# Seven products instead of eight in the last matrix product, and a new order of pairs and weights in the stage ahead of it

## The chip, the cores and the metric

The kernel runs on one core of a Trainium2 chip. The metric is the device time of one execution in microseconds (us); the kernel before takes 1808.94 us (median of three runs, 1808.52 to 1811.02). TensorE (PE) multiplies matrices into PSUM, which has eight banks of 128x512 floats. ScalarE (ACT), VectorE (DVE) and GpSimd (POOL) prepare operands and clear PSUM. SyncE (SP) issues every DMA, in order. Each engine executes its own queue in the order in which the program was written.

## The reference

Attention with pooled keys and values feeds a first network, `_moe_ref`, and this a second one, `_moe2_ref`. The change touches the second alone, for 4608 tokens, 512 features and 1536 inner columns:

```python
def _moe2_ref(x, w_gate, w_val, w_out) -> np.ndarray:
    g = x @ w_gate
    silu = g * (1.0 / (1.0 + np.exp(-g)))
    val = x @ w_val
    return (silu * val @ w_out).astype(np.float32)
```

Weights arrive as 64-bit floats and are turned into 32-bit floats on the chip (`bits_ops`).

## The kernel before

Every product is computed from a high and a low part: an operand is split into `hi` (a rounded copy, made on ACT or DVE) and `lo` (the rest, a subtraction on DVE or POOL), and three matmuls (hi·hi, hi·lo, lo·hi) stand for one. Tokens are in nine tiles of 512.

Stage 1, to about 978 us, is attention and the first network. Stage 2, the gate stage, follows to 1511.85 us. There two token tiles make a pair; tile 8 is left over and makes a half pair of two pieces of 256 tokens. For a pair and one of six groups `g` of inner columns, the four products of a 2x2 block matrix (gate and value, for two token tiles) are computed by Strassen's scheme in Winograd's form as seven products (`PRODUCTS`): the left operands A11, A12, S1, S2, S3, A22, S4 are tokens or sums of them (`x_ops`), the right ones are weights or differences of them, prepared once in stage 1 by `conv2_ops` and kept in DRAM (`wdr`). Each of the seven takes 12 matmuls in a group (`pair_ops`). The weights of groups 0 to 2 stay in SBUF (21 slots, list `res`), those of groups 3 to 5 are loaded anew for every pair into four buffers X0 to X3 (`ring_load`), four products ahead. `u_ring` has eight tiles that take results out of PSUM; a finished tile goes to DRAM (`sdr`), and its buffer is free when the store has landed. Pairs run 0, 1, 2, 3, half; groups 0 to 5.

Stage 3 multiplies the results by `w_out` in the plain way: for each tile, 12 blocks `f` of inner columns, four blocks of features, three matmuls: 9·12·4·3 = 1296 of 512 columns, line 455 (`out_ops`, `mm3`). Its weights were split by `conv3_ops` (12 stores `wodr` of 512 KB) and are loaded at the end of the gate stage into the 12 first slots of `res`.

A list scheduler inside the program (`Plan`) writes the order of all queues. Each operation has a due time, alternatives by engine with assumed durations, and the operations it depends on; the scheduler takes what can start first, and among near equals what is due first. So an operation of low urgency runs as soon as its inputs and buffers are there. `at(when, ...)` sets only in which order buffers are handed out.

SBUF slots come from a lower and an upper region (`low`, and `const` or `al_p`). Token operands of stage 2 lie in the lower one (`x_ring`, 18 slots), as do X0 to X3 and the last two of the 21 slots; the other 19 slots lie in the upper.

Of the kernel before, what the change touches and what calls it, by code (L numbers as in the profile page):

```python
# [8 lines left out]
F32 = mybir.dt.float32  # L9
# [29 lines left out]
for _c in CHUNKS:  # L39
    for _t in range(2):  # L40
# [139 lines left out]
def tile_pooled_attention_moe_moe2(  # L180
# [358 lines left out]
    def conv2_ops(due, f):  # L539
        g, par = divmod(f, 2)  # L540
        (ta, ka), (tb, kb), (tg, kg), (tv, kv) = st_all[0:4]
        bits_ops(due, w_gate[f], kv_ring, Ring([(ta, ka), (tb, kb), (tg, kg)]))
        bits_ops(due, w_val[f], kv_ring, Ring([(ta, ka), (tb, kb), (tv, kv)]))
        h0, h1 = slice(0, 256), slice(256, 512)
        src = {"G1": (tg[:, h0], kg), "G2": (tg[:, h1], kg), "V1": (tv[:, h0], kv), "V2": (tv[:, h1], kv),
               "T1": (ta[:, h0], ka), "T2": (ta[:, h1], ka), "T3": (tb[:, h0], kb), "T4": (tb[:, h1], kb)}
        for o, x, y in (("T1", "V1", "G1"), ("T2", "V2", "T1"), ("T3", "V2", "V1"), ("T4", "G2", "T2")):
            (to, ko), (tx, kx), (ty, ky) = src[o], src[x], src[y]
            op(due, [e(256, lambda E=E, to=to, tx=tx, ty=ty: E.tensor_tensor(out=to, in0=tx, in1=ty, op=ALU.subtract))
                     for e, E in ((pool, P), (lambda n, fn: dve(n, fn, True), V))], [kx, ky], [ko])  # L550
# [70 lines left out]
    def pair_start(p, g):  # L621
        return P2S + p * NFP * P2D + g * (P2D if 2 * p + 1 < NTILE else P2L)

    scr = {}

    def pair_ops(p, g, j):
        n = TT if 2 * p + 1 < NTILE else TT // 2
        full = n == TT
        step = (P2D if full else P2L) / NPR
        k = p * NFP + g  # L630
        b1, b2, b3 = TURN[2 * k % 3], (5, 6), TURN[(2 * k + 1) % 3]

        def dst(i, f):
# [1 line left out]

        x, _, acc, first = PRODUCTS[j]
        for a in range(2):
            d = pair_start(p, g) + (j + 0.5 * a) * step
# [4 lines left out]
            for kk in range(2):  # L643
                kx, gx = xslot[p, x, kk]

                def product(kk=kk, bk=bk, gx=gx, gw=gw, a=a, first=first):
                    for q, (i0, i1) in enumerate(((0, 0), (0, 1), (1, 0))):
                        c = 256 * a + 128 * kk
                        nc.tensor.matmul(out=bk, lhsT=gw()[:, i0, c:c + 128], rhs=gx()[:, i1, 0:n],  # L649
                                         start=first and kk == 0 and q == 0, stop=kk == 1 and q == 2,  # L650
                                         skip_group_check=True)

                op(d, [pe(680 * n / TT, product)], [kw + "h", kw + "l", kx + "h", kx + "l"], [kb])
# [36 lines left out]
    out_slot = {}  # L690

    def out_ops(due, t, f, ring):
        (y, Y), (kg, gg) = ys_ring(), ring()
        keys = [f"sdr{t // 2}_{t % 2}_{f}"] if t < NTILE - 1 else [f"sdr{t // 2}_{i}_{f}" for i in range(2)]
        op(due - 1.5, [dma(1 << 18, lambda: sync.dma_start(out=ys(y), in_=sdr[t][f]))], keys, [Y])
        op(due - 0.5, [act(512, False, lambda: A_.copy(out=gg()[:, 0, :], in_=ys(y))),
                       dve(512, lambda: V.tensor_copy(out=gg()[:, 0, :], in_=ys(y)), True, 2)], [Y], [kg + "h"])
        op(due - 0.5, [dve(512, lambda: V.tensor_tensor(
            out=gg()[:, 1, :], in0=ys(y), in1=gg()[:, 0, :].bitcast(F32), op=ALU.subtract), True),
            pool(512, lambda: P.tensor_tensor(  # L700
                out=gg()[:, 1, :], in0=ys(y), in1=gg()[:, 0, :].bitcast(F32), op=ALU.subtract))],
           [Y, kg + "h"], [kg + "l"])
        kw, gw = out_slot[f]
        for dt in range(4):
            bi = 4 * (t % 2) + dt
            op(due, [pe(680, lambda dt=dt, bi=bi: mm3(
                bank[bi], gw(), slice(dt * 128, dt * 128 + 128), gg(), f == 0, f == NF2 - 1))],
               [kw + "h", kw + "l", kg + "h", kg + "l"], [f"bank{bi}"])
        if f == NF2 - 1:
            for dt in range(4):  # L710
                (z, Z), bk, kb = o_ring(), bank[4 * (t % 2) + dt], f"bank{4 * (t % 2) + dt}"
                op(due, [act(512, True, lambda z=z, bk=bk: A_.copy(out=z, in_=bk)),
                         dve(512, lambda z=z, bk=bk: V.tensor_copy(out=z, in_=bk))], [kb], [Z])
                op(due, [dma(1 << 18, lambda z=z, dt=dt: sync.dma_start(
                    out=outT[dt, :, t * TT:(t + 1) * TT], in_=z))], [Z], [f"out{t}_{dt}"])

    o_ring = Ring(st_all)


    groups = []  # L720
# [80 lines left out]
    for p in range(NP2):  # L801
        for q in range(2 * NPR):
            kk, o = divmod(q, NPR)
            if p == 0:
                w = LAST + 3.0 + 4.5 * kk + 0.6 * o
            else:
                w0 = pair_start(p - 1, NFP - 1)
                w = w0 + 0.01 if q < XSPARE else max(w, w0 + P2D / NPR * ((q - XSPARE) % NPR + 1) + 0.01)
            at(w, x_ops, w, p, kk, o, x_ring)
        for g in range(NFP):  # L810
            step = (P2D if 2 * p + 1 < NTILE else P2L) / NPR
            s0 = pair_start(p, g)
            if g >= RES:
                for j in range(NPR):
                    at(s0 + (j - 3.9) * step, ring_load, s0 + (j - 4) * step, g, j)
            for j in range(NPR):
                at(s0 + j * step, pair_ops, p, g, j)
    last = [wslot_k for _, wslot_k in res]
    for f in range(NF2):
        out_slot[f] = last[f]  # L820
        w = pair_start(NP2 - 1, f // NPR + 1) + 0.1
        at(w, load_ops, w, out_slot[f], wodr[f], [f"wodr{f}"])
    g_ring = Ring(last[NF2:n_up])
    for t in range(NTILE):
        for f in range(NF2):
            w = P3S + P3D * (t * NF2 + f)
            at(w, out_ops, w, t, f, g_ring)

    with tc.manual_schedule():
        A_.preload_act_table_set("natural_log_exp_and_others")  # L830
# [49 lines left out]
```

## Time and profile before

| | |
|---|---|
| median of three runs | 1808.94 us |
| the profiled execution | 1811.45 us |
| its span, first to last instruction | 1809.7 us |
| mean granted clock | 0.99 |
| PE busy | 1752.4 us (97%) |
| DVE, ACT, POOL busy | 1204.9, 1014.1, 468.0 us |
| DMA moved | 255.31 MB |

The profile comes from one execution, whose own time stands in the second row; 1.75 us of it lie outside the span. Times in the rows below count from the start of the span. A matmul's shown duration overlaps that of the next, so the pace is read from the starts of successive rows.

### The profile page before, as it was taken

To read this page: it belongs to the slowest core of one execution; us is meant where nothing else is said; L and a number is where in the kernel's file an instruction comes from. 1 tells how busy PE (TensorE), PEld (TensorE's weight loads), DVE (VectorE), ACT (ScalarE), POOL (GpSimd) and SP (SyncE) were. 2 spreads that over 40 slices of the span, in tenths; PEclk is the share of its full clock that TensorE was granted. 3 is DMA by queue.
4 is the path that set the end of the run, shared out by engine and by line. 5 is a ranking of instruction groups with operands and counts; after the bars stand their busy time and mean duration, and the time that the engine had idled before them with its cause. 6 is when DMAs were issued, how large, how long until landed. Compare 5 with 4: busy or idle time off the path is not lost.

```text
span 1809.7 us, 23566 instructions
## 1 busy us (share of the span) xinstructions
PE 1752.4 (97%) x8136; PEld 1414.1 (78%) x8136; DVE 1204.9 (67%) x1933; ACT 1014.1 (56%) x2184; POOL 468.0 (26%) x370
## 2 busy tenths in 40 slices
PE   5899899999999999999999999999999999999999
PEld 3577667787778877777888887888878888888887
DVE  7899988989889898988998435363453542222221
ACT  7777777778777777777876334343343332322222
POOL 4556542536443343524543001010000000000000
PEclk9799999999999999999999999999999999999999
DMA  8412353424132331313257374381653895434432
GB/s 273 145 41 82 113 158 104 133 71 145 48 126 88 104 120 55 122 35 134 95 196 268 134 248 141 132 275 47 221 186 104 268 325 188 144 118 122 142 120 70
DMA packets 117816, 255.31 MB, mean 141 GB/s; under 512 B 12224, under 2 KB 36800, under 8 KB 117696
## 3 DMA queue, kind: packets, MB, share of 16 engines
q1 hardware_dynamic: 117696, 253.81, 42.4%
q8 instruction: 64, 1.05, 0.2%
q14 instruction: 56, 0.46, 0.1%
HBM read 176.16 MB, written 77.59 MB: 140 GB/s over the span
## 4 chain that ended last, share of the span: by engine, by line
PE 83%; DVE 7%; DMA 5%; ACT 3%; issue 1%; POOL 1%; SPq 0%; DVEq 0%; ACTq 0%; POOLq 0%
PE bank L455 52%; PE bank L649 26%; PE bank L437 2%; PE bank L384 2%; PE bank L421 1%; DVE SC L517 1%; DVE G L514 1%; DMA ys_vps<-ydr 1%; DMA RAW<-in_k 1%; DVE SA L520 1%; DMA RAW<-in_v 1%; DMA X<-wdr 1%; DVE SA L509 1%; ACT QS L399 1%; DVE bank L510 0%
## 5 line engine op out<-in xcount | busy, mean ns | idle before, releaser
L455 PE MATMUL bank<-G,W 128*128 128x512 f32 x2088 | 515.0, 394 | 0.6 <-POOL W L324 0.6
L455 PEld LDWEIGHTS bank<-G,W 128*128 128x128 f32 x2088 | 387.3, 188 | 86.7 <-issue 5.2
L455 PE MATMUL bank<-X,W 128*128 128x512 f32 x1728 | 444.6, 402 | 7.3 <-DVE SA L520 7.1
L455 PEld LDWEIGHTS bank<-X,W 128*128 128x128 f32 x1728 | 322.9, 191 | 91.5 <-DVE SA L520 13.7
L506 POOL TENSOR_TENSOR SC<-SC,SB 128x512 f32<-128x512 f32 x144 | 201.9, 1402 | 290.3 <-ACT SC L504 288.6
L649 PE MATMUL bank<-W,X 128*128 128x512 f32 (+1 forms) x972 | 216.2, 367 | 5.9 <-DMA X<-wdr 3.0
L649 PEld LDWEIGHTS bank<-W,X 128*128 128x128 f32 x972 | 168.8, 188 | 38.4 <-ACT SA L658 1.8
L649 PE MATMUL bank<-W,W 128*128 128x512 f32 (+1 forms) x828 | 184.3, 367 | 0.4 <-ACT SB L658 0.4
L455 PE MATMUL bank<-W,W 128*128 128x512 f32 x756 | 174.0, 389 | 0.0
L649 PEld LDWEIGHTS bank<-W,W 128*128 128x128 f32 x828 | 143.8, 188 | 27.3 <-ACT SB L658 0.6
L455 PEld LDWEIGHTS bank<-W,W 128*128 128x128 f32 x756 | 141.9, 188 | 29.4
L512 ACT ACTIVATE SB<-SC,qc 128x512 f32<-128x512 f32 x144 | 104.8, 727 | 65.2 <-POOL SC L506 64.6
L514 DVE SCALAR_TENSOR_TENSOR G<-bank,ab,SB 128x512 fp32r<-128x512 f32 x144 | 107.2, 745 | 41.5 <-PE bank L455 28.6
L503 ACT ACTIVATE SB<-bank 128x512 f32<-128x512 f32 x144 | 86.3, 599 | 66.0 <-DVE G L525 41.2
L504 ACT ACTIVATE SC<-SB,babs 128x512 f32<-128x512 f32 x144 | 117.8, 818 | 0.1
L517 DVE SCALAR_TENSOR_TENSOR SC<-SC,G 128x512 f32<-128x512 f32 x144 | 114.0, 792 | 2.6
L507 ACT ACTIVATE SA<-bank,ab 128x512 f32<-128x512 f32 x144 | 112.3, 780 | 0.1
L510 DVE SCALAR_TENSOR_TENSOR bank<-SA,ab,bank 128x512 f32<-128x512 f32 x144 | 107.5, 747 | 1.3
L520 DVE SCALAR_TENSOR_TENSOR SA<-bank,ab,SC 128x512 f32<-128x512 f32 x144 | 106.6, 741 | 0.4
L320 POOL TENSOR_TENSOR ST<-ST,ST 128x512 int32<-128x512 int32 x53 | 77.0, 1453 | 114.0 <-DVE ST L317 78.4
L509 DVE TENSOR_TENSOR SA<-SA,bank 128x512 f32<-128x512 f32 x144 | 97.5, 678 | 10.3 <-ACT SA L507 9.6
L399 ACT ACTIVATE QS<-bank,MX 128x72 f32<-128x72 f32 x272 | 83.8, 325 | 35.1 <-DVE MX L395 35.1
(182 smaller groups left out, 2243.5 us busy)
## 6 DMA issues: line engine op xcount, KB each, us to landing
X<-wdr SPq DMA_DIRECT2D x105, 512.0 KB
wdr<-ST SPq DMA_DIRECT2D x84, 256.0 KB
ydr<-ST SPq DMA_DIRECT2D x44, 256.0 KB
RAW<-in_w_out SPq DMA_DIRECT2D x19, 512.0 KB
RAW<-in_k SPq DMA_DIRECT2D x32, 288.0 KB
RAW<-in_v SPq DMA_DIRECT2D x32, 288.0 KB
W<-wdr SPq DMA_DIRECT2D x18, 512.0 KB
ys_vps<-sdr SPq DMA_DIRECT2D x36, 256.0 KB
```

The costliest lines, as they stand in the source:

```text
L399: A_.activation(out=ss[:, 4 * i + j, :], in_=src[:, j, :], func=AF.Exp, bias=mx[:, 4 * i + j, :], accum_out=sm[:, 4 * i + j, :])
L455: nc.tensor.matmul(out=out, lhsT=w[:, i0, wc], rhs=x[:, i1, :], start=first and j == 0, stop=last and j == 2)
L504: op(d, [act(512, False, lambda: A_.activation(out=C, in_=Bt, func=AF.Identity, scale=babs[:, 1:2], bias=babs[:, 0:1]), 2)], [kB, "ab"], [kC])
L506: op(d, [pool(512, lambda: P.tensor_tensor(out=C, in0=C, in1=Bt, op=ALU.mult))], [kB], [kC])
L507: op(d, [act(512, True, lambda: A_.activation(out=A, in_=hb, func=AF.Identity, scale=ab[:, 3:4], bias=ab[:, 2:3]), 2)], [kh, "ab"], [kA])
L509: op(d, [dve(512, lambda: V.tensor_tensor(out=A, in0=A, in1=hb, op=ALU.mult))], [kh], [kA])
L510: op(d, [dve(512, lambda: V.scalar_tensor_tensor(out=hb, in0=A, scalar=ab[:, 1:2], in1=hb, op0=ALU.add, op1=ALU.mult), ptrs=1)], [kA], [kh])
L512: op(d, [act(512, False, lambda: A_.activation(out=Bt, in_=C, func=AF.Ln, bias=qc), 1)], [kC], [kB])
L514: op(d, [dve(512, lambda: V.scalar_tensor_tensor(out=gt[:, 0, :], in0=hb, scalar=ab[:, 0:1], in1=Bt, op0=ALU.add, op1=ALU.mult), ptrs=1)], ...
L517: op(d, [dve(512, lambda: V.scalar_tensor_tensor(out=C, in0=C, scalar=QC, in1=gt[:, 0, :].bitcast(F32), op0=ALU.add, op1=ALU.mult), True)] ...
L520: op(d, [dve(512, lambda: V.scalar_tensor_tensor(out=A, in0=hb, scalar=ab[:, 0:1], in1=C, op0=ALU.add, op1=ALU.subtract), ptrs=1)], [kC, k ...
L649: nc.tensor.matmul(out=bk, lhsT=gw()[:, i0, c:c + 128], rhs=gx()[:, i1, 0:n], start=first and kk == 0 and q == 0, stop=kk == 1 and q == 2, ...
```

## The change

- **Output products by the same scheme.** `conv3_ops` takes two blocks of `w_out` at a time and prepares seven right operands per group (`seven_ops`, now shared with `conv2_ops`): 42 stores of 256 KB take the place of 12 of 512 KB, through two half buffers (`late_ring`). `left3_ops` loads results from `sdr`, builds S1 to S4 and splits all seven left operands; `out_ops` does seven products per pair, each of 36 matmuls (two feature blocks, six groups, three parts), 1008 matmuls of 512 columns and 252 of 256. The 18 slots of `x_ring` hold the split operands of three products. The loads of left operands have rings of six buffers: K1 (A21), K2 (A22, then S), K3 (A11) and T (A12, A22, and A12 once more).
- **Gate stage.** The half pair runs fourth, pair 3 last. In these two the groups run 3, 0, 4, 1, 5, 2, so that a streamed group stands next to a resident one. Output weights are loaded (`load3_ops`) into each resident slot once pair 3 has used it for the last time.

```diff
+P2SEQ = (0, 1, 2, 4, 3)
+GSEQ = tuple((0, 1, 2, 3, 4, 5) if i < 3 else (3, 0, 4, 1, 5, 2) for i in range(NP2))
...
-    wodr = [dr_p.tile([128, 1024], F32, name=f"wodr{f}") for f in range(NF2)]
+    wodr = [[dr_p.tile([128, 2, 256], F32, name=f"wodr{g}_{j}") for j in range(NPR)] for g in range(NFP)]
...
+    rawf = [r.bitcast(F32).rearrange("p a t -> p (a t)") for r in RAW]
+    halves = [(rawf[i][:, 512 * c:512 * c + 512], f"raw{i}{'ab'[c]}") for i in range(NRAW) for c in range(2)]
+    late_ring = Ring(halves[4:6])
...
+    def conv3_ops(due, g):
+        a, b, t0, t1 = st_all[0:4]
+        bits_ops(due, w_out2[2 * g], late_raw, Ring([a, b, t0]))
+        bits_ops(due, w_out2[2 * g + 1], late_raw, Ring([a, b, t1]))
+        seven_ops(due, (t0, t1), ((0, 0), (1, 0), (0, 1), (1, 1)), (a, b), late_ring,
+                  lambda j: (wodr[g][j], f"wodr{g}_{j}"))
...
+        sums = {"S1": ("S", "A21", "S", ALU.add), "S2": ("S", "S", "A11", ALU.subtract),
+                "S3": ("A21", "A11", "A21", ALU.subtract), "S4": ("S", "T", "S", ALU.subtract)}
...
+                    for q, (i0, i1) in enumerate(((0, 0), (0, 1), (1, 0))):
+                        c = 256 * i0 + 128 * d
+                        nc.tensor.matmul(out=bk, lhsT=gw()[:, g % 2, c:c + 128], rhs=gx()[:, i1, 0:n],
+                                         start=first and g == 0 and q == 0, stop=g == NFP - 1 and q == 2,
+                                         skip_group_check=True)
```

PE at the start of the output stage, first in the kernel before. Names are output, token operand, weights; W3, W5, W7 are slots of the upper region, X4 to X7 and the first W of each row after lie in the lower.

```order
L649 MATMUL bank3_137<-W20_1175,X0_76 128x512 x3
L455 MATMUL bank0_134<-W27_1588,W3_118 128x512 x3
L455 MATMUL bank1_135<-W27_1588,W3_118 128x512 x3
L455 MATMUL bank2_136<-W27_1588,W3_118 128x512 x3
L455 MATMUL bank3_137<-W27_1588,W3_118 128x512 x3
L455 MATMUL bank0_134<-W29_1689,W5_119 128x512 x3
```

The same place in the changed kernel:

```order
L668 MATMUL bank3_137<-W20_1205,W28_1658 128x512 x3
L769 MATMUL bank0_134<-W22_1291,W3_118 128x512 x3
L769 MATMUL bank0_134<-W24_1408,W3_118 128x512 x3
L769 MATMUL bank0_134<-X4_80,W5_119 128x512 x3
L769 MATMUL bank0_134<-X5_81,W5_119 128x512 x3
L769 MATMUL bank0_134<-X6_82,W7_120 128x512 x3
L769 MATMUL bank0_134<-X7_83,W7_120 128x512 x3
L769 MATMUL bank1_135<-W22_1291,W3_118 128x512 x3
```

A bank now takes six groups in a row; one product needs six token operands, and weights of the upper region meet token operands of the lower.

ACT in the first pair of the gate stage, before: copies out of PSUM (L658), silu (L671, L679), and the preparation of the output weights (L532 makes a `hi` part; RAW2 is the buffer that is stored).

```order
L658 COPY SA0_95<-bank2_136 128x512
L532 CAST RAW2_103<-ST2_106 128x512
L658 COPY SA1_96<-bank3_137 128x512
L658 COPY SB0_97<-bank2_136 128x512
L658 COPY SB1_98<-bank3_137 128x512
L679 ACTIVATE bank2_136<-bank2_136 128x512
L679 ACTIVATE bank3_137<-bank3_137 128x512
L658 COPY SC0_99<-bank0_134 128x512
```

The same place after (L677 is the copy, L541 the `hi` part):

```order
L677 COPY SA0_95<-bank2_136 128x512
L541 CAST RAW2_103<-ST2_106 128x256
L677 COPY SA1_96<-bank3_137 128x512
L677 COPY SB0_97<-bank2_136 128x512
L541 CAST RAW2_103<-ST3_107 128x256
L321 ACTIVATE ST2_106<-RAW0_101 128x512
L677 COPY SB1_98<-bank3_137 128x512
L541 CAST RAW2_103<-ST0_104 128x256
L698 ACTIVATE bank2_136<-bank2_136 128x512
L698 ACTIVATE bank3_137<-bank3_137 128x512
L541 CAST RAW2_103<-ST0_104 128x256
L677 COPY SC0_99<-bank0_134 128x512
```

Such casts now stand between the copies up to the end of the third group: 22 of them on ACT from the first copy of the first pair on, 4 before.

SP in the half pair, before: W<-wodr loads output weights, sdr8 takes the half pair's results.

```order
L687 DMA sdr6_211<-SB1_98 128x512
L567 DMA W3_118<-wodr0_193 128x1024
L567 DMA W5_119<-wodr1_194 128x1024
L567 DMA W7_120<-wodr2_195 128x1024
L567 DMA W9_121<-wodr3_196 128x1024
L567 DMA W11_122<-wodr4_197 128x1024
L681 DMA sdr8_213<-SC0_99 128x256
L681 DMA sdr8_213<-SC1_100 128x256
L687 DMA sdr8_213<-SA0_95 128x256
L687 DMA sdr8_213<-SA1_96 128x256
L567 DMA W13_123<-wodr5_198 128x1024
```

SP in the half pair after, from its first stores on (X<-wdr loads streamed weights: group, then product):

```order
L700 DMA sdr8_243<-SA0_95 128x256
L584 DMA X0_76<-wdr4_2_181 128x1024
L700 DMA sdr8_243<-SA1_96 128x256
L706 DMA sdr8_243<-SC0_99 128x256
L706 DMA sdr8_243<-SC1_100 128x256
L584 DMA X1_77<-wdr4_3_182 128x1024
L608 DMA ys_vps_6796<-ydr6_148 128x512
L700 DMA sdr8_243<-ST4_108 128x256
L700 DMA sdr8_243<-ST5_109 128x256
L584 DMA X2_78<-wdr4_4_183 128x1024
L706 DMA sdr8_243<-SB0_97 128x256
```

The loads of output weights are gone from this stretch; they now come in pair 3.

## Rows read from the trace of the kernel before

**Rows 1.** The page, busy time by engine (us, share of span, instructions).
```profile
PE 1752.4 (97%) x8136; PEld 1414.1 (78%) x8136; DVE 1204.9 (67%) x1933; ACT 1014.1 (56%) x2184; POOL 468.0 (26%) x370
```
**Rows 2.** Busy time in four stretches (PE, PEld, DVE, ACT, POOL, clock, DMA).
```profile
985.00:1004.00 19.00, 19.00 (x84) 15.38 (x83) 11.14 (x19) 9.72 (x17) 3.46 (x3) 1.00 0.97 364
1329.00:1443.30 114.30, 114.30 (x503) 94.25 (x502) 49.67 (x81) 39.94 (x71) 1.29 (x2) 1.00 0.49 164
1443.30:1511.90 68.60, 63.23 (x506) 60.73 (x505) 28.34 (x69) 25.10 (x65) 2.15 (x2) 1.00 0.92 326
1511.90:1805.80 293.90, 293.90 (x1297) 243.09 (x1296) 74.42 (x112) 78.57 (x128) 0.00 (x0) 1.00 0.38 116
```
**Rows 3.** Chain that ended last, from 1443 us (start us, us, what).
```profile
1444.96 5.09 DMA sdr<-SB
...
1476.73 4.33 DMA sdr<-SC
...
1499.97 5.75 DMA X<-wdr
...
1512.01 293.81 PE bank L455 x1296
...
1805.88 0.59 ACT ST L712
```
**Rows 4.** Timeline of PE (start us, us, engine line op).
```profile
1245.42 9.09 PE L649 MATMUL bank<-W,W 128*128 128x512 f32 x39
1254.35 0.85 PE L649 MATMUL bank<-X,W 128*128 128x512 f32 x3
...
1445.79 3.34 PE L649 MATMUL bank<-W,W 128*128 128x256 f32 x27
1448.97 0.52 PE L649 MATMUL bank<-X,W 128*128 128x256 f32 x3
...
1475.99 0.52 PE L649 MATMUL bank<-X,X 128*128 128x256 f32 x3
1476.35 0.52 PE L649 MATMUL bank<-W,X 128*128 128x256 f32 x3
```
**Rows 5.** Groups by line and shape, 1100 to 1805 us (busy us, mean ns).
```profile
L663 DVE TENSOR_TENSOR SC<-SC,bank 128x512 f32<-128x512 f32 x28 | 19.0, 685 | 37.0 <-ACT SC L658 26.5 <-PE bank L649 8.2 <-ACT SC L671 2.0
L698 DVE TENSOR_TENSOR W<-ys_qs,W 128x512 fp32r<-128x512 f32 x23 | 15.8, 692 | 42.6 <-ACT W L696 42.6
...
L663 DVE TENSOR_TENSOR SB<-SB,bank 128x256 f32<-128x256 f32 x10 | 4.2, 418 | 10.0 <-ACT SB L658 10.0
...
L696 ACT CAST W<-ys_qs 128x512 fp32r<-128x512 f32 x23 | 14.3, 624 | 44.4 <-PE bank L455 44.0 <-PE bank L649 0.4
L658 ACT COPY SA<-bank 128x512 f32<-128x512 f32 x26 | 15.3, 587 | 33.9 <-PE bank L649 33.9
```
**Rows 6.** Timeline of SP: stores of gate operands, then the last stores of all.
```profile
711.77 11.91 SPq L555 DMA_DIRECT2D wdr<-ST  x5
...
737.41 13.04 SPq L555 DMA_DIRECT2D wdr<-ST  x4
...
813.66 16.60 SPq L555 DMA_DIRECT2D wdr<-ST  x7
...
1804.41 2.42 SPq L714 DMA_DIRECT2D outT<-ST  x4
```
**Rows 7.** Waits of PE, 1443 to 1512 us (us in total, times, longest).
```profile
PE bank L649 <- DMA X<-wdr: 3.0, 4, 1.3
PE bank L649 <- ACT SC L658: 1.1, 1, 1.1
```
**Rows 8.** Waits of PE in the full pairs, 1000 to 1443 us.
```profile
PE bank L649 <- ACT SA L658: 1.0, 2, 0.6
PE bank L649 <- ACT SB L658: 0.8, 2, 0.4
PE bank L649 <- ACT ST L658: 0.3, 1, 0.3
```

More of the change, by code (lines that the diff above doesn't have):

```diff
@@ L687, in pair_ops @@
                 op(d, [dma(512 * n, lambda t=t, f=f: sync.dma_start(out=dst(0, f), in_=t))], [kt], [f"sdr{p}_0_{f}"])
[L690 to L715, printed above, removed]
@@ L717, in tile_pooled_attention_moe_moe2, with s_load, left3_ops @@
-    o_ring = Ring(st_all)
+    rings3 = {}
+    s_live, a_slot, out_slot = {}, {}, {}
+    def s_load(due, p, nm, g, ring):
+        y, Y = rings3[ring]()
+        i, f = int(nm[1]) - 1, 2 * g + int(nm[2]) - 1
+        n = TT if 2 * p + 1 < NTILE else TT // 2
+        src = sdr[2 * p + i][f] if n == TT else sdr[2 * p][f][:, n * i:n * i + n]
+        op(due, [dma(512 * n, lambda: sync.dma_start(out=y()[:, 0:n], in_=src))], [f"sdr{p}_{i}_{f}"], [Y])
+        return lambda: y()[:, 0:n], Y
+    def left3_ops(due, p, j, g, slot):
+        n = TT if 2 * p + 1 < NTILE else TT // 2
+        nm, live = PRODUCTS[j][0], s_live.setdefault((p, g), {})
+        ld = due - 1.0
+        if nm == "A11":
+            live["A11"] = s_load(ld, p, "A11", g, "K3")
+        elif nm == "S1":
+            live["A21"], live["S"] = s_load(ld, p, "A21", g, "K1"), s_load(ld, p, "A22", g, "K2")
+        elif nm != "S2" and nm != "S3":
+            live["T"] = s_load(ld, p, "A12" if nm == "S4" else nm, g, "T")
+        sums = {"S1": ("S", "A21", "S", ALU.add), "S2": ("S", "S", "A11", ALU.subtract),
+                "S3": ("A21", "A11", "A21", ALU.subtract), "S4": ("S", "T", "S", ALU.subtract)}
+        if nm in sums:
+            (o, O), (x, X_), (y, Y), what = *(live[q] for q in sums[nm][:3]), sums[nm][3]
+            op(due, [e(n, lambda E=E: E.tensor_tensor(out=o(), in0=x(), in1=y(), op=what))
+                     for e, E in ((pool, P), (lambda n, fn: dve(n, fn, True), V))], [X_, Y], [O])
+        src, K = live[sums[nm][0] if nm in sums else "A11" if nm == "A11" else "T"]
+        k, get = a_slot[p, j, g] = slot
+        hi, lo = lambda: get()[:, 0, 0:n], lambda: get()[:, 1, 0:n]
+        op(due, [act(n, False, lambda: A_.copy(out=hi(), in_=src())),
+                 dve(n, lambda: V.tensor_copy(out=hi(), in_=src()), True, 2)], [K], [k + "h"])
+        op(due, [dve(n, lambda: V.tensor_tensor(out=lo(), in0=src(), in1=hi().bitcast(F32), op=ALU.subtract), True),
+                 pool(n, lambda: P.tensor_tensor(out=lo(), in0=src(), in1=hi().bitcast(F32), op=ALU.subtract))],
+           [K, k + "h"], [k + "l"])
@@ new lines, in load3_ops, with out_ops, product, copy @@
+    def load3_ops(due, j, g):
+        k, get = out_slot[j, g // 2]
+        c = g % 2
+        op(due, [dma(1 << 18, lambda: sync.dma_start(
+            out=get().bitcast(F32)[:, c, :], in_=wodr[g][j].rearrange("p h c -> p (h c)")))],
+           [f"wodr{g}_{j}"], [k + "hl"[c]])
+    def out_ops(p, j):
+        n = TT if 2 * p + 1 < NTILE else TT // 2
+        step = P3D if n == TT else P3L
+        _, _, acc, first = PRODUCTS[j]
+        b = [((3 * p + q) % 4 * 2, (3 * p + q) % 4 * 2 + 1) for q in range(3)]
+        for d in range(2):
+            due = P3B[p] + (j + 0.5 * d) * step
+            bi = b[acc][d]
+            bk, kb = bank[bi][:, 0:n], f"bank{bi}"
+            for g in range(NFP):
+                kx, gx = a_slot[p, j, g]
+                kw, gw = out_slot[j, g // 2]
+                def product(g=g, bk=bk, gx=gx, gw=gw, d=d):
+                    for q, (i0, i1) in enumerate(((0, 0), (0, 1), (1, 0))):
[3 more added lines that the diff above has]
+                                         skip_group_check=True)
+                op(due + 0.08 * step * g, [pe(680 * n / TT, product)], [kw + "hl"[g % 2], kx + "h", kx + "l"], [kb])
+            due += 0.5 * step
+            def copy(nm, bk=bk, kb=kb, due=due):
+                t, kt = u_ring()
+                scr[nm, d] = (t[:, 0:n], kt)
+                op(due, [act(n, True, lambda: A_.copy(out=t[:, 0:n], in_=bk)),
+                         dve(n, lambda: V.tensor_copy(out=t[:, 0:n], in_=bk))], [kb], [kt])
+            def add(nm, bi, due=due):
+                t, kt = scr[nm, d]
+                op(due, [dve(n, lambda: V.tensor_tensor(out=t, in0=t, in1=bank[bi][:, 0:n], op=ALU.add))],
+                   [f"bank{bi}"], [kt])
+            def store(nm, i, dt, due=due):
+                t, kt = scr[nm, d]
+                c = (2 * p + i) * TT if n == TT else 2 * p * TT + n * i
+                op(due, [dma(512 * n, lambda: sync.dma_start(out=outT[dt, :, c:c + n], in_=t))], [kt], [f"out{c}_{dt}"])
+            if j == 0:
+                copy("t0")
+            elif j == 1:
+                add("t0", bi)
+                store("t0", 0, d)
+            elif j == 3:
+                copy("v0")
+            elif j == 4:
+                copy("t1")
+                add("t1", b[2][d])
+                store("t1", 1, 2 + d)
+            elif j == 5:
+                copy("z")
+                store("z", 1, d)
+            elif j == 6:
+                add("v0", bi)
+                store("v0", 0, 2 + d)
@@ L816, in tile_pooled_attention_moe_moe2 @@
             for j in range(NPR):
[L817 to L827, printed above, removed]
+                at(s0 + j * step, pair_ops, i, c, j)
```

113 lines of the change are left out of this document (77 added, 36 removed).

## The prediction

> **What bounds the kernel now.** I read the page first: PE is busy 97% of the span [rows 1]. Then the stretches: in the last full pair and in the output stage PE fills its stretch, while DVE fills 49.67 of 114.3 us and 74.42 of 293.9 us [rows 2]; there the matmuls themselves are the time. The half pair is different: PE stands still for part of it, and the DMA engines are busy 0.92 of the time at 326 GB/s [rows 2]. The chain of waits says the same: from 1512.01 us it is one piece of 1296 matmuls, 293.81 us, and in the half pair it hops over DMA landings of 4.3 to 5.75 us [rows 3]. Last I read the pace of matmuls from the starts of successive rows. 39 matmuls of 512 columns with weights from the upper region and tokens from the lower take 1254.35 - 1245.42 = 8.93 us, 0.2290 us each [rows 4]; the output stage before has both operands in the upper region and takes 293.81/1296 = 0.2267 [rows 3]. With 256 columns it is (1448.97 - 1445.79)/27 = 0.1178 for weights from the upper region, and (1476.35 - 1475.99)/3 = 0.120 for streamed ones [rows 4]. The granted clock is 1.00, its upper level of 2.4 GHz, in all these stretches [rows 2]; I take it to stay.
>
> **Output stage.** Removed: 293.8 us. Added: per full pair 7 products of 36 matmuls, 252. By slots 19/21 of them (228) have weights of the upper region, so 0.2290, and 24 have 0.2267: 52.2 + 5.4 = 57.65 us; four pairs 230.6. The half pair has 252 of 256 columns, 29.7 us. Sum 260.3, **a gain of 33.5 us**, if nothing makes PE wait.
>
> The Trainium skill, page "TensorE: Matmul & The Clock Gate", section "Wait — 56ns, not 53.3ns?", puts the pace of a warm matmul at columns/2.4 GHz plus about 2.5 ns, thus 0.2158 and 0.1092 us. The rows here are 5 to 8% above that. By the page the gain would be 1296·0.2158 - 1008·0.2158 - 252·0.1092 = 34.6 us, an estimate 1.1 us above mine.
>
> What covers the added work: a full pair needs on DVE 42 `lo` parts, 20 of the 24 sums (the order gives the rest to POOL) and 6 adds from PSUM, 68 operations of at most 0.692 us [rows 5], 47 us beside 57.65; on ACT 42·0.624 + 8·0.587 = 31 us. DMA per pair: 36 loads and 8 stores of 256 KB, 11.5 MB in 57.65 us, 200 GB/s, under the 326 that the half pair moved [rows 2]. The 18 operand slots let the split work run up to two products, 16 us, ahead of PE, and a landing takes 4.3 to 5.8 [rows 3]. PE's accumulators are copied 4 us (half a product) before they are written again; a copy takes 0.59. So I expect little waiting: 1 us with the entry into the stage, bounds 0 and 4.
>
> The end gets shorter: before, four copies and four stores of 256 KB stand behind the last matmul, and 1809.7 - 1805.8 = 3.9 us pass [rows 3, 6]; after, one add of 0.42 and a store of 128 KB: -0.5 us.
>
> **Half pair.** It took 68.6 us [rows 2]; its 504 matmuls need 252·0.1178 + 252·0.120 = 59.9. Of the 8.7 lost, 3.0 are waits for streamed weights and 1.1 one wait for a result buffer (SC) whose store landed late [rows 3, 7]. The change takes 12 loads of 512 KB of output weights and the first loads of the output stage out of it; left are 21·0.52 + 24·0.13 MB of results + 8·0.26 of the next pair's tokens = 16.2 MB, 271 GB/s. Group order 3, 0, 4, 1, 5, 2 gives the first four loads of a streamed group a resident group's 9.9 us. But the last three can start only when the group's own products free a buffer: product 4's load starts after 12·0.118 = 1.4 us and is needed at 5.65. With 4.2 us to land, a landing of 5.75 [rows 3] costs 1.5 us per streamed group, 4.5 in all; a landing under 4.2 costs nothing. The long landings come from the fullest stretch; nearer the lower end I take 1.7. **Gain 7.0 us**, bounds 4.2 and 8.7.
>
> **Half pair to pair 3.** 14 operands of a full pair must now be split beside a group of 9.9 us instead of 19: 14 `lo`s and about 8 sums at 0.69 plus 10 operations of the group at 0.42 are 19.4 us on DVE; the new pair's first products (2.7 us each) give some of that time. The three full transitions before cost 2.1 us together [rows 8]. I add 1.0, bounds 0 and 19.4 - 9.9 - 2·2.7 = 4. In pair 3, streamed weights (11 MB), output weights (11), results (6.3) and first operands come to about 250 GB/s, no more than the half pair; each output load follows the product that frees its slot. Nothing added there.
>
> **Output weights (conv3).** 42 splits of 256 columns and stores of 256 KB replace 12 of 512 columns. Half of them run in tile 8 of stage 1, which has no attention work left, as their like, the 84 stores `wdr`, run in the tiles before it; nothing is set for that half. The rest stands in ACT's order in the first three groups of pair 0: 22 casts in 57 us, one per 2.6. Behind a cast that waits for its buffer stand PSUM copies, and PE wants the bank again after six matmuls, 1.4 us. The nearest rows for the pace of such a loop of two buffers are 16.60 us for seven stores and 11.91 for five, less the last issue (0.5): 2.7 and 2.85 us a store [rows 6]. 22·(2.85 - 2.6) = 5.5 us; if landings are as quick as assumed, nothing. The start of this stretch is full of other DMA (364 GB/s [rows 2]), so not nothing: **2.5 us lost**, bounds 0 and 5.7. A gain is excluded but for the 2.1 us of [rows 8], partly of this place.
>
> The Trainium skill, page "DMA: Bandwidth & Descriptors", section "Anatomy of one DMA — SWDGE (gpsimd) path", gives a DMA of that path about 2.0 us + bytes/436e3, 2.6 us for 256 KB. By that estimate the loop would need 1.7 us a store and this term would be nil; the rows of stage 1 are slower.
>
> **Sum**, against the profiled execution of 1811.45 us: -33.5 - 7.0 - 0.5 + 1.0 + 1.0 + 2.5 = -36.5. The median shown is 2.5 us under that execution: 1808.94 - 36.5 = 1772.4, **1772 us**.
>
> **Rivals.**
> - *Refills of T on the path (slower).* T's six buffers hold A12, A22 and A12 in turn, and SP is one strict queue in which these loads stand among stores that wait for DVE. If a refill starts only when PE is at the product before, its landing of about 5.1 us (the SB store of [rows 3]) shows twice per pair: 2·5·5.1 = 51 us, 1823 us. For it: six buffers for three uses. Against it: A22's split needs only the slot of a product three back, so the refill has 16 us. It decides from the point where the lead of 18 slots falls under one product, 8.2 us. Chance 0.04.
> - *DVE sets the pace in S1 to S4.* A product with sums needs 6 `lo`s, 6 sums, 1 add: 13·0.69 = 9.0 us against PE's 36·0.2290 = 8.2, for the half 13·0.418 = 5.4 against 4.2 [rows 5]. Three in a row overdraw 2.4 and 3.6 us a pair. If the lead of 16 us isn't there, 4·2.4 + 3.6 = 13: 1785 us. Against: the average is 47 of 57.65. Chance 0.07.
> - *The half pair's stall stays.* Were the streaming itself and not the output weights the cause, 7.0 us come back: 1779. The waits of [rows 7] for X<-wdr speak for it, the 6.3 MB taken out against. Chance 0.08.
> - *conv3 throttles pair 0.* One row shows four stores in 13.04 us, 4.2 each [rows 6]; at that pace 22·(4.2 - 2.6) = 35 us and 1805, no change. That row is of stage 1, where DVE is much fuller. Chance 0.03.
> - *My forecast* has the rest, 0.78.
>
> **Range and chances.** Without any of the waits that I added or left, and with 0.2267 for the output stage, it would be 1772 - 2.5 - 1 - 1 - 1.7 - 2.3, about 1764. With each at its upper bound 1772 + 3.2 + 3 + 3 + 2.8 = 1784. 1764 to 1784 leaves out T, DVE and conv3 and a little of the forecast. What a measurement can tell from no change is 0.2%, 3.6 us: faster 0.94 (forecast, DVE, half pair, a third of conv3), the same 0.02, slower 0.04.
>
> **What would show it.** The output stage: PE full, 252 matmuls in 57 to 58 us, with the two paces of [rows 4], and DVE at about 0.8. The half pair: 60 to 63 us, DMA share well under 0.92. Pair 0 of the gate stage: a few PE waits for L677 copies behind L541 casts, gone from the fourth group on. It is wrong if PE waits in the output stage for casts or `lo`s (DVE), if SP sits before a T load (T), or if waits for X<-wdr stay at 3 us and more.

## The result, and the profile after

The changed kernel takes 1779.5 us (median of four runs, 1777.7 to 1781.7) against 1810.0 beside it, a ratio of 0.983 (95% interval 0.9815 to 0.9849): 30.5 us faster. That is inside the range, 7.5 us above the forecast of 1772, and on the number of the rival "the half pair's stall stays" (1779). The profiled execution took 1777.68 us, its span 1775.9.

First the output stage, pair by pair (columns as in [rows 2]; the last stretch ends with the kernel):

```profile
1512.22:1569.90 57.68, 57.68 (x254) 47.37 (x253) 46.61 (x71) 30.38 (x51) 6.17 (x4) 1.00 0.69 236
1569.90:1627.50 57.60, 57.60 (x254) 47.30 (x253) 46.33 (x70) 30.46 (x51) 5.12 (x4) 1.00 0.62 201
1627.50:1685.20 57.70, 57.70 (x254) 47.40 (x253) 46.55 (x70) 30.57 (x51) 5.14 (x4) 1.00 0.61 199
1685.20:1742.80 57.60, 57.60 (x254) 47.30 (x253) 40.47 (x77) 26.35 (x49) 1.53 (x3) 1.00 0.43 136
1742.80:1775.90 33.10, 29.78 (x253) 29.57 (x251) 15.92 (x42) 11.69 (x33) 0.61 (x1) 1.00 0.20 65
```

PE is full in every pair, a pair takes 57.6 to 57.7 us, and DVE is busy at most 46.6 of them. Then the chain that ended last (start us, us, what), answering to [rows 3]:

```profile
766.06 13.95 PE bank L464 x60
...
1333.58 5.16 DMA X<-wdr
...
1344.01 4.86 DMA sdr<-SC
...
1356.99 5.23 DMA X<-wdr
...
1365.71 4.69 DMA sdr<-SA
...
1401.44 6.34 DMA X<-wdr
...
1512.38 260.21 PE bank L769 x1260
```

The output stage is one piece, 260.21 us in place of 293.81, but it begins where it began before, near 1512 us. The half pair, now from 1329.9 us, still hops over landings, of weight loads (X<-wdr) and of result stores (sdr) in turn. PE's waits there, 1329 to 1400 us (us in total, times, longest), beside [rows 7]:

```profile
PE bank L668 <- ACT SC L677: 2.4, 2, 1.3
PE bank L668 <- DMA X<-wdr: 2.3, 3, 1.0
PE bank L668 <- ACT SA L677: 0.7, 1, 0.7
```

The view behind [rows 7] has two more waits:

```profile
PE bank L649 <- ACT ST L658: 0.6, 1, 0.6
PE bank L649 <- ACT SB L658: 0.4, 1, 0.4
```

So before the change PE waited 2.1 us for copies into result buffers, not 1.1, beside 3.0 us for weights. The chain of [rows 3] has two more hops between those shown, and with them three result stores stand in it ahead of two weight loads:

```profile
1465.35 4.67 DMA sdr<-ST
...
1487.32 5.71 DMA X<-wdr
```

The DMA share of the half pair fell from 0.92 to 0.75, but that is a mean. While three of the landings in the changed kernel's chain were under way (columns as in [rows 2]), the DMA engines were busy nearly all the time:

```profile
1333.60:1338.70 5.10, 3.77 (x31) 3.40 (x29) 2.62 (x6) 2.72 (x7) 0.00 (x0) 1.00 1.02 341
1344.00:1348.90 4.90, 4.23 (x37) 4.02 (x36) 1.31 (x4) 0.84 (x2) 0.00 (x0) 1.00 0.91 256
1357.00:1362.20 5.20, 4.62 (x37) 4.24 (x36) 0.84 (x2) 1.72 (x6) 0.00 (x0) 1.00 0.98 314
```

To see where time went, I put marks into the two traces: M, a row of 60 matmuls of stage 1 near 767 us, which is in every trace (`766.06 13.95` above; 769.87 in the kernel before); E, the start of stage 1's last three matmuls; H, the start of the half pair's first matmul; O, the start of the output stage. In PE's timeline (columns as in [rows 4]) of the kernel before, E, the start of pair 3, the half pair's start (there after pair 3) and O:

```profile
989.11 0.86 PE L455 MATMUL bank<-G,W 128*128 128x512 f32 x3
...
1328.57 14.58 PE L649 MATMUL bank<-W,W 128*128 128x512 f32 x63
...
1443.32 0.52 PE L649 MATMUL bank<-X,W 128*128 128x256 f32 x3
...
1511.85 8.35 PE L455 MATMUL bank<-W,W 128*128 128x512 f32 x36
```

and of the changed one:

```profile
991.44 0.86 PE L464 MATMUL bank<-G,W 128*128 128x512 f32 x3
...
1324.43 9.91 PE L668 MATMUL bank<-W,X 128*128 128x512 f32 x60
...
1512.22 1.53 PE L769 MATMUL bank<-W,W 128*128 128x512 f32 x6
```

The row at 1324.43 us mixes sizes: by its length it holds 24 matmuls of 512 columns and 36 of 256, so H is 1324.43 + 24·0.2267 = 1329.9. Before, pair 2 ends where pair 3 begins, at 1328.57. H of the runs below is found the same way where a row mixes.

| stretch | before | after | difference |
|---|---|---|---|
| start to M | 769.9 | 766.1 | -3.8 |
| M to E, the end of stage 1 | 219.2 | 225.4 | +6.1 |
| E to the end of pair 2 | 339.5 | 338.5 | -1.0 |
| half pair and pair 3, in either order, to O | 183.3 | 182.3 | -1.0 |
| output stage | 294.0 | 260.4 | -33.6 |
| after the last matmul | 3.9 | 3.3 | -0.6 |

The first line is not the change's: no instruction differs there, and over all the runs below M stands anywhere from 764.4 to 772.6 us. Without it the two profiles differ by 30.0 us, as the medians do.

The other surprise of the table is +6.1 at the end of stage 1. Busy times from 885 to 990 us in the kernel before (columns as in [rows 2]):

```profile
885.00:990.00 105.00, 105.00 (x459) 85.89 (x458) 96.95 (x142) 78.13 (x124) 49.61 (x35) 1.00 0.58 197
```

and in the changed one:

```profile
885.00:990.00 105.00, 101.04 (x437) 81.36 (x436) 99.13 (x147) 72.75 (x120) 54.42 (x43) 1.00 0.59 195
```

PE's waits of the changed kernel, 900 to 990 us; the kernel before has none there:

```profile
PE bank L464 <- DVE SA L529: 3.6, 2, 2.1
PE bank L668 <- DVE SA L529: 0.4, 1, 0.4
```

DVE was already busy 97 of 105 us. It now takes 99, and twice it is so late with the activation of stage 1 that PE stands.

### The profile page after: what moved, and what is told of

It reads as the page before. It is cut to its first block, busy times and chain, and to the rows that moved or that the text cites. A ratio compares the mean times of both kernels' runs of the same rounds, so it can differ in the third digit from the quotient of the medians.

```text
span 1775.9 us, 24384 instructions
## 1 busy us (share of the span) xinstructions
PE 1715.5 (97%) x8100; PEld 1386.9 (78%) x8100; DVE 1356.4 (76%) x2204; ACT 1075.7 (61%) x2319; POOL 506.7 (29%) x406
## 4 chain that ended last, share of the span: by engine, by line
PE 80%; DVE 10%; DMA 5%; ACT 2%; issue 2%; POOL 1%; SPq 0%; DVEq 0%; ACTq 0%; POOLq 0%
PE bank L464 35%; PE bank L668 25%; PE bank L769 15%; PE bank L393 2%; PE bank L446 2%; PE bank L430 2%; DVE SC L526 1%; DMA ys_vps<-ydr 1%; DVE G L523 1%; DVE SA L529 1%; DMA X<-wdr 1%; DMA RAW<-in_k 1%; DVE SA L518 1%; DVE W L629 1%; DVE bank L519 1%
## 5 line engine op out<-in xcount | busy, mean ns | idle before, releaser
L464 PE MATMUL bank<-G,W 128*128 128x512 f32 x1728 | 430.9, 395 | 0.6 <-POOL W L333 0.6
L464 PEld LDWEIGHTS bank<-G,W 128*128 128x128 f32 x1728 | 319.7, 188 | 72.6 <-issue 5.2
L668 PE MATMUL bank<-W,W 128*128 128x512 f32 (+1 forms) x828 | 185.6, 367 | 1.8 <-ACT SC L677 1.1
L769 PE MATMUL bank<-W,W 128*128 128x512 f32 (+1 forms) x840 | 175.7, 366 | 0.0
L526 DVE SCALAR_TENSOR_TENSOR SC<-SC,G 128x512 f32<-128x512 f32 x144 | 117.1, 814 | 3.0
L529 DVE SCALAR_TENSOR_TENSOR SA<-bank,ab,SC 128x512 f32<-128x512 f32 x144 | 106.8, 742 | 0.4
L518 DVE TENSOR_TENSOR SA<-SA,bank 128x512 f32<-128x512 f32 x144 | 97.6, 679 | 9.9 <-ACT SA L516 9.5
```

The source lines that it names most:

```text
L464: nc.tensor.matmul(out=out, lhsT=w[:, i0, wc], rhs=x[:, i1, :], start=first and j == 0, stop=last and j == 2)
L518: op(d, [dve(512, lambda: V.tensor_tensor(out=A, in0=A, in1=hb, op=ALU.mult))], [kh], [kA])
L526: op(d, [dve(512, lambda: V.scalar_tensor_tensor(out=C, in0=C, scalar=QC, in1=gt[:, 0, :].bitcast(F32), op0=ALU.add, op1=ALU.mult), True)] ...
L529: op(d, [dve(512, lambda: V.scalar_tensor_tensor(out=A, in0=hb, scalar=ab[:, 0:1], in1=C, op0=ALU.add, op1=ALU.subtract), ptrs=1)], [kC, k ...
L668: nc.tensor.matmul(out=bk, lhsT=gw()[:, i0, m:m + 128], rhs=gx()[:, i1, 0:n], start=first and kk == 0 and q == 0, stop=kk == 1 and q == 2, ...
L769: nc.tensor.matmul(out=bk, lhsT=gw()[:, g % 2, c:c + 128], rhs=gx()[:, i1, 0:n], start=first and g == 0 and q == 0, stop=g == NFP - 1 and ...
```

## The experiments

Times are medians beside the kernel before on the same chip. Since the start scatters by 8 us, I read M to O, 746.2 us in the changed kernel and 742.0 before, as well. The last column is the half pair from its first matmul to its last, without six matmuls of the next stretch that stand among them; before the change it is 68.5. Both come from one execution of each kernel.

| kernel | median us | ratio (95% interval) | M to O | half pair |
|---|---|---|---|---|
| changed | 1779.5 | 0.9832 (0.9815 to 0.9849) | 746.2 | 66.4 |
| half pair fifth | 1782.2 | 0.9851 (0.9832 to 0.9870) | 750.5 | 69.9 |
| streamed groups first | 1783.5 | 0.9855 (0.9827 to 0.9883) | 748.1 | 68.3 |
| twelve result buffers | 1776.5 | 0.9822 (0.9798 to 0.9845) | 742.0 | 61.0 |
| half pair without streaming | 1772.0 | 0.9794 (0.9775 to 0.9813) | 741.4 | 59.6 |
| conversion after stage 1 | 1775.0 | 0.9820 (0.9797 to 0.9844) | 745.3 | 67.6 |
| no conversion | 1770.4 | 0.9784 (0.9769 to 0.9799) | 738.3 | 63.7 |
| three edits together | 1773.0 | 0.9799 (0.9775 to 0.9823) | 743.1 | 63.9 |
| before, twelve result buffers | 1811.3 | 1.0004 (0.9990 to 1.0017) | 740.0 | 68.8 |

**The gate stage's order.** My theory was that the new order had given nothing, the rival that it had given the 6 us of the prediction.

```diff
-P2SEQ = (0, 1, 2, 4, 3)
-GSEQ = tuple((0, 1, 2, 3, 4, 5) if i < 3 else (3, 0, 4, 1, 5, 2) for i in range(NP2))
+P2SEQ = (0, 1, 2, 3, 4)
+GSEQ = tuple((0, 1, 2, 3, 4, 5) for i in range(NP2))
```

> The changed kernel with the gate stage's order put back (half pair fifth, groups 0 to 5 in turn); output stage and output weights stay changed. Theory (the move gave almost nothing: half pair and pair 3 together take 182.5 us after and 182.8 before): 1779 to 1782 us, at most 2 above the changed kernel. Rival (the move gave the 6 us of the prediction, and something else lost them): 1785 to 1787 us.

> The changed kernel with the half pair fourth, but groups 0 to 5 in turn in it and in pair 3. Theory (the half pair stands still for result buffers and for loads queued behind stores on SP, which the group order does not touch): 1779 to 1781 us. Rival (the resident groups between give the streamed weights their time, as the prediction had it): 3 to 5 us above the changed kernel, 1783 to 1785 us, with waits for X<-wdr over 5 us in the half pair.

They took 1795.4 and 1799.9 us, far above either number, and answer another question. A last group that is streamed still needs X0 to X3 when the output stage puts its first operands there, so part of both is overwritten, and PE waits for the hand-over (12.6 us for X<-sdr in the second). The order is thus also what sets those four buffers free. So the place was put back alone:

```diff
-P2SEQ = (0, 1, 2, 4, 3)
+P2SEQ = (0, 1, 2, 3, 4)
```

> The changed kernel with only the order of the pairs put back: half pair fifth, groups 3, 0, 4, 1, 5, 2 in it and in the pair before it, so that its last group is a resident one and the four streaming buffers X are free for the output stage. Theory (the place is worth little, what the half pair stands still for is the loop of SP's queue and its result buffers): 1779 to 1782 us. Rival (the new output stage's first loads, 11 MB of weights and 18 operands, cost the half pair more than the old ones did): 1784 to 1790 us.

1782.2 us, at the upper end of the theory's range, and M to O 4.3 us longer. The half pair took 69.9 us there (1446.22 to 1516.1, the six output matmuls in its midst taken off). By these readings the place is worth some 3 to 4 us beside the new output stage; the intervals of the two medians overlap, so the size is not proven.

The half pair alone in turn, pair 3 alternating:

```diff
-GSEQ = tuple((0, 1, 2, 3, 4, 5) if i < 3 else (3, 0, 4, 1, 5, 2) for i in range(NP2))
+GSEQ = tuple((0, 1, 2, 3, 4, 5) if i < 4 else (3, 0, 4, 1, 5, 2) for i in range(NP2))
```

> The changed kernel with groups 0 to 5 in turn in the half pair alone (fourth, as changed); pair 3 keeps 3, 0, 4, 1, 5, 2. Theory (the alternation does nothing for the half pair): half pair and pair 3 take 182 to 184 us as with it (182.5), 1779 to 1781 us. Rival (resident groups between give streamed weights their time): waits for X<-wdr grow from 2.3 to over 5 us, 1782 to 1785 us.

1791.1 us, but no answer for a like reason: here the first loads of pair 3 take buffers that the half pair's last, streamed group has not read, and part of its result comes from other weights. The clean form ends on resident groups:

```diff
-GSEQ = tuple((0, 1, 2, 3, 4, 5) if i < 3 else (3, 0, 4, 1, 5, 2) for i in range(NP2))
+GSEQ = ((0, 1, 2, 3, 4, 5),) * 3 + ((3, 4, 5, 0, 1, 2), (3, 0, 4, 1, 5, 2))
```

> The changed kernel with the half pair's groups in the order 3, 4, 5, 0, 1, 2: still fourth and ending on a resident group, but its three streamed groups stand one behind the other. Theory (a streamed group needs a resident one beside it: 21 loads of 512 KB in 30 us would be 367 GB/s, more than the 326 that the old half pair moved): waits for X<-wdr grow from 2.3 us to 8 and more, half pair and pair 3 take 188 us and more instead of 182.5, 1785 us and more. Rival (the group order is worth nothing; the result buffers set the half pair's time in any order): 182 to 184 us, 1779 to 1781 us.

1783.5 us, a median between theory and rival, with half pair and pair 3 at 183.1. PE's waits, 985 to 1530 us, of which the half pair has those for X<-wdr alone:

```profile
PE bank L668 <- DMA X<-wdr: 6.7, 7, 1.7
PE bank L668 <- ACT ST L677: 1.0, 2, 0.8
PE bank L668 <- DVE SA L678: 0.7, 1, 0.7
```

Waits for weights grew from 2.8 us (2.3 in the half pair, 0.5 in pair 3) to 6.7, less than my theory's 8, and yet the stretch is only 0.8 us longer: the waits for ACT's copies that stood in the half pair, 3.1 us, are not there any more. One wait covers the other, and by that stretch the rival's 182 to 184 us fit.

**Result buffers.** If so, taking one away alone must show the other.

```diff
+    u_more = Ring(u_ring.items + st_all[0:4])
...
-                t, kt = u_ring()
+                t, kt = (u_more if i == 3 else u_ring)()
```

> The changed kernel with twelve result buffers instead of eight in the half pair (ST0 to ST3, idle there, join the ring). Theory (3.1 us of the half pair's standstill are copies that wait for a buffer whose store took 4.7 to 4.9 us to land): no wait for ACT's L677 copies is left in the half pair, its time with pair 3 falls from 182.5 by about 3, 1776 to 1777 us. Rival (behind them the streamed weights are late anyway): waits for X<-wdr take their place, 1779 to 1780 us.

Half pair and pair 3 fell from 182.3 to 176.9 us, 5.4 where 3 were expected, in one execution of each. PE's waits, 1331 to 1515 us:

```profile
PE bank L669 <- DMA X<-wdr: 1.6, 4, 0.7
PE bank L669 <- DVE SA L683: 0.2, 1, 0.2
```

No copy is awaited any more, the chain has no result store left in the half pair, and here the weights are not later but earlier. A reason that fits, and was not tried by itself: behind a store that waits for its data stand the next weight loads on SP's queue (the load at 1333.58 us above was issued right behind such a store), and stores are late where copies are. The median is 3 us lower, which its interval doesn't prove; M to O, read from one execution, is 4.2 us shorter. Streaming removed instead:

```diff
-            kw, gw = wslot[g, j]
+            kw, gw = wslot[g % RES if i == 3 else g, j]
...
-            if g >= RES:
+            if g >= RES and i != 3:
```

> The half pair's groups 3 to 5 take the resident weights of groups 0 to 2, so its 21 loads of streamed weights are left out and part of its result is another one. Theory (loads behind stores on SP's queue and the stores' landings beside them make the stall): the half pair falls to 60 to 61.5 us, with pair 3 to 175 to 177 instead of 182.5, 1772 to 1774 us. Rival (the result buffers alone make it): 3 us of waits for L677 stay, 1776 to 1777 us.

174.8 us with pair 3, 1772.0 us: as my theory had it. PE waits for ACT's copies 0.2 us there. So in these two traces either edit alone takes most of the stall: it needs both, the streamed loads and the few buffers. (The better version below gained less from the buffers.) In the kernel before the same twelve buffers:

```diff
-                t, kt = u_ring()
+                t, kt = (u_ring if full else u_more)()
```

> The kernel before with twelve result buffers instead of eight in its half pair, nothing else. Theory (the result buffers held its half pair too, but there the weight loads are late by themselves, at a DMA share of 0.92): the waits for L658 copies (2.1 us) go, those for X<-wdr stay at 3 or grow; the half pair falls from 68.6 to 65 or 67 us, 1806 to 1808 us. Rival (the result buffers are the whole cause): 62 to 63 us, 1803 to 1804. Rival (the weight loads are the whole cause, as the prediction had it): no change, 68 to 69 us.

No change: 1811.3 us, the half pair 68.8 (1438.24 to 1507.08) after 68.5. Waits of PE, 700 to 1815 us:

```profile
PE bank L650 <- DMA X<-wdr: 6.7, 7, 1.7
PE bank L650 <- ACT SB L659: 0.8, 2, 0.5
PE bank L650 <- ACT ST L659: 0.4, 1, 0.4
```

There the copies' waits in the half pair fell from 2.1 to 0.5 us, and the waits for weights grew from 3.0 us [rows 7] to 6.7: the weight loads are late by themselves. The waits went as the theory had it, but the time fits the last rival, the one that argued as the prediction did.

**The conversion of the output weights.**

```diff
-    at(P2S - 1, lambda: op(P2S - 1, [("NONE", 0, 0, False, lambda: None)], [], ["raw2"] + [k for _, k in halves[4:]]))
+    at(P2S + 3.9, lambda: op(P2S - 1, [("NONE", 0, 0, False, lambda: None)], [f"ydr{NTILE - 1}_3"],
+                           ["raw0", "raw1", "raw2"] + [k for _, k in halves[4:]]))
```

> The changed kernel with the output weights' conversion held back until the last tile of stage 1 is stored. Theory (in tile 8 its work takes time on a DVE that is 96% busy, and PE waits there 3.6 us for it): those waits are gone and pairs 0 to 2 carry the 42 splits with at most 2.5 us lost: 1774.5 to 1777 us. Rival (the conversion costs the same wherever it stands, by its loop of two buffers on ACT's and SP's queues): no change against the changed kernel, 1779 to 1782, the waits now in pairs 0 to 2.

M to E went back to 219.3 us, as before the change, and E to H grew from 338.5 to 342.8: 6.1 won, 4.3 lost, and the next stretch lost 0.9 more. In pairs 0 to 2 PE now waits 3.7 us for ACT's copies, 0.6 in the changed kernel. By M to O the rival is right, no change to speak of; the median of 1775.0, over runs from 1770 to 1783, can't decide. DVE's groups, 885 to 990 us (columns as in [rows 5], the idle time behind them), of the changed kernel and of this one:

```profile
L526 DVE SCALAR_TENSOR_TENSOR SC<-SC,G 128x512 f32<-128x512 f32 x18 | 17.1, 949 | 0.7
L529 DVE SCALAR_TENSOR_TENSOR SA<-bank,ab,SC 128x512 f32<-128x512 f32 x18 | 13.3, 741 | 0.0
...
L534 DVE TENSOR_TENSOR G<-SA,SB 128x512 fp32r<-128x512 f32 x15 | 12.3, 821 | 0.0
L518 DVE TENSOR_TENSOR SA<-SA,bank 128x512 f32<-128x512 f32 x17 | 11.5, 676 | 0.8 <-ACT SA L516 0.8
```
```profile
L526 DVE SCALAR_TENSOR_TENSOR SC<-SC,G 128x512 f32<-128x512 f32 x18 | 13.7, 760 | 0.9
...
L534 DVE TENSOR_TENSOR G<-SA,SB 128x512 fp32r<-128x512 f32 x18 | 13.5, 747 | 0.2
L529 DVE SCALAR_TENSOR_TENSOR SA<-bank,ab,SC 128x512 f32<-128x512 f32 x18 | 13.4, 746 | 0.1
...
L518 DVE TENSOR_TENSOR SA<-SA,bank 128x512 f32<-128x512 f32 x17 | 11.6, 682 | 2.2 <-ACT SA L516 2.2
```

The conversion doesn't only add operations to DVE. It also lengthens those that have both inputs in SBUF (L526 from 760 to 949 ns, L534 from 747 to 821), while those with an input in PSUM stay (L529, L518); POOL is busy 54 us of this stretch instead of 35. The price of all of it (only this hunk is printed; the loads of the output stage change too):

```diff
...
-    for g in range(NFP):
-        w = P2S + 4 + 9 * g
-        at(w, conv3_ops, w + 1, g)
```

> The conversion of the output weights is left out altogether; the output stage loads 256 KB blocks of the gate weights in their place, so only its time has a meaning. Theory: the 4.9 us that tile 8 lost come back, 1774 to 1775 us. Rival (tile 8's waits come from the order of the other work on DVE): 1778 to 1780 us.

1770.4 us: M to E 219.7, E to H 339.1, O 7.8 us earlier against M. Of that 5.7 us are at the end of stage 1; the rest shows in half pair and pair 3 (179.6). The theory was short by what lies past stage 1. The end of stage 1 is the firm part: M to E is 225.4 to 227.0 us in all nine traces in which the changed conversion starts in tile 8, and 219.2 to 219.7 in the other five, the two of the kernel before among them.

**Lead of the output stage.**

```diff
-                slot = x_ring.items[(2 * NPR * NP2 + pos) % len(x_ring.items)]
+                slot = x_ring.items[(2 * NPR * NP2 + pos % 12) % len(x_ring.items)]
```

> The changed kernel with 12 instead of 18 operand slots in the output stage, so that DVE's split work can run one product (8 us) ahead of PE instead of two. Theory (DVE overdraws 2.4 us in the three products with sums and makes it good in the other four; a lead of 8 us still covers that): output stage 260 to 263 us. Rival (the lead of 16 us is what hides DVE): PE waits for L742 parts in every pair, 265 to 275 us.

260.21 us for the stage, to the digit (1777.3 us, a single run). But this doesn't test the lead: operands are still handed out two products ahead, so with twelve slots they are written over ones not yet read, and the work runs as early as before. That the lead of two products is what hides DVE stays unshown. The run serves as a second one of the changed gate stage: half pair and pair 3 took 183.0 us, with 3.3 us of waits for copies and 2.9 for weights.

**A better version.** Held-back conversion with four staging buffers (RAW1 and RAW2) and twelve result buffers. RAW1 is taken from the loads of raw weights, which keep RAW0 alone; the lines of the other two experiments stand beside these:

```diff
-    late_raw = Ring(raw_all[0:2])
+    late_raw = Ring(raw_all[0:1])
...
-    late_ring = Ring(halves[4:6])
+    late_ring = Ring(halves[2:6])
...
```

> Three edits to the changed kernel together: the conversion of the output weights held back until stage 1 is stored, four staging buffers for it instead of two, and twelve result buffers in the half pair. Theory: tile 8 gives back 6 us and the half pair 5, as each alone did, and the four staging buffers bring the 4.3 us that the held-back conversion lost in pairs 0 to 2 down to 1: 1768 to 1770 us. Rival (the conversion costs pairs 0 to 2 by its casts in ACT's queue, not by its buffers): 4 us stay, 1772 to 1774 us.

1773.0 us, ratio 0.980: the lowest median of the kernels that compute everything, some 6 us under the changed kernel by ratio, though the intervals overlap, and 3 us by M to O. The rival's number fits. E to H is 341.8, so four staging buffers gave back 1 of the 4.3 us. PE's waits, 1331 to 1515 us:

```profile
PE bank L669 <- DMA X<-wdr: 4.2, 4, 1.6
PE bank L669 <- ACT W L627: 0.9, 1, 0.9
PE bank L669 <- ACT SC L678: 0.6, 1, 0.6
PE bank L669 <- DVE SA L683: 0.2, 1, 0.2
```

Here the half pair and pair 3 take 182.0 us, not 176.9, although no copy waits in the half pair (the 0.6 us for SC stand near the end of pair 3). Three of the four loads that were late are the same ones as with twelve buffers alone, each by 0.4 to 1.3 us more; the pair issued at 1400.57 us was awaited until 1407.29, there from 1400.39 to 1405.93. Whether that is the one execution or the moved conversion is open. Beside the held-back conversion with eight buffers (183.3) the twelve are worth 1.3 us, so the 5.4 above is no firm size: what the traces agree on is that with twelve buffers no copy waits in the half pair, and that late weights are then most of what is left.

## Why the prediction was right, and where not

- **Output stage, -33.5 and +1.0 for waits: right.** -33.6. The two paces of [rows 4] gave 57.65 us a pair, measured 57.6 to 57.7; no wait at all stood in the stage, so 1.0 was too careful. The rivals on T and on DVE are out: DVE's 46.6 us a pair is the 47 worked out, and nothing of it reached PE. (One reading was off without effect: the rows stand 5 to 10% above 0.2158 and 0.1092, not 5 to 8, since 0.120 is 10% above 0.1092.)
- **The end, -0.5:** -0.6.
- **Half pair, -7.0, and its transition, +1.0: the step that failed.** Together -6.0 expected, -1.0 measured. The half pair takes 66.4 us, not 61.6, and pair 3 after it about 1 us more than before. The step booked all of the 8.7 us but 1.7 as late weight loads that would go with the output weights' 6.3 MB. It put the waits for result buffers at nothing without a reason, and it saw 1.1 us of them where the trace had 2.1. They stayed: 3.1 us, beside 2.3 for weights. The buffers come free when their stores have landed, and stores on the chain still took 4.7 to 4.9 us: the step reasoned with a mean (271 GB/s; 247 measured), but while those stores landed the DMA engines were busy 0.91 and 0.86 of the time. The same holds for the weight loads, 5.2 us on the chain where 4.2 would have cost nothing. In all four traces with eight buffers, this gate stage and streaming (the changed kernel, twelve operand slots, held-back conversion, no conversion) result stores stand on the chain of the half pair; in the two with twelve none does. In one of these half pair and pair 3 took 176.9 us, about what was forecast; in the other 182.0. So that the buffers hold the half pair is shown, and what they cost, between 1 and 5 us, is not settled. What alternation and place are worth with eight is about 1 and 4 us, by one execution each.
- **Output weights, +2.5 in pair 0: wrong place, size doubled.** +6.1 at the end of stage 1, -1.0 in pairs 0 to 2, together +5.1. "Nothing is set for that half" failed: I took tile 8 to have room since attention was over, without its own window of DVE. The stretch shows DVE at 97 of 105 us before the change. A cost in pairs 0 to 2 came only where the experiments moved the conversion there.
- **Sum.** -36.5 expected; -1.1 from the stage, -0.1 from the end, +5.0 and +2.6 from the two terms make -30.1, and the medians -30.5. The rival "the half pair's stall stays" hit the time by luck: 5.0 us of stall that stayed and 2.6 us from the conversion, which it didn't have, add up to about its 7. Of the cause it has a part: streaming is needed for the stall, but so are the few buffers.

## What to carry to other kernels

When a stretch stalls on one resource, list what waits next before its whole loss is booked as gain: here the waits for result buffers stood in the trace before the change and were left when the bytes went, and twelve buffers gave a different answer before and after the change. A mean share of the DMA engines says little about one landing: look at the share while that landing is under way. A loop with a landing in it is judged by buffers times time per use against landing time, and is worth computing anew wherever the work per buffer halves; that sum was not made here ahead of the change. "Fills a gap" needs the busy time of the engine in that very stretch, and of POOL where DVE's operations have both inputs in SBUF.

## What was not expected of the hardware

- DVE operations with both inputs in SBUF get longer when POOL is busier: 760 to 949 ns on average, with single ones of 1.78 us, while forms with a PSUM input stay (741 and 746, 676 and 682). Taken one by one in stage 1 of the changed kernel, the 51 L526 operations that no POOL operation overlaps took 684 ns on average and 696 at most, the 93 that one overlaps 885 on average; L529, which reads a bank, took 744 and 741. The Trainium skill, page "SBUF — State Buffer", section "🔬 SBUF: two separate sides", says that a DVE operation with two SBUF inputs and a POOL operation that reads SBUF take a shared port pair in turn and the other one blocks; these numbers agree.
- The granted clock in the first 400 us differs between executions of the same instructions: 0.97 from 200 to 300 us in the kernel before, 1.00 in the changed one, 0.89 from 216 to 256 us in the held-back conversion. M moved by up to 8 us among fourteen profiles: over those 400 us the clock was 0.97 where M came first (764.4 us) and 0.94 where it came last (772.6 us), and from there to M it was 1.00 in both. Runs of the held-back conversion scatter by 13 us; how much of that is the clock is not shown.
- Weight loads of 512 KB that stand on the chain took 5.2 us to land in the changed half pair and 6.3 us just behind it, beside 5.7 and 5.75 in the half pair before, although the mean DMA share fell from 0.92 to 0.75. While each of the three in the changed kernel was under way the share was 0.98 or more. How long such a load takes at a low share is not read here, since the chain shows only the landings that something waits for.
